# A planned instruction order replaced by another: attention with a position bias and a two-layer MoE-style MLP on one core

## The chip, the cores and the metric

The kernel runs on one core of one Trainium2 chip. The metric is the time of one execution on the device in microseconds (us), of which the median of three runs is taken. Engines are named as the profile names them: PE is TensorE (PEld its weight loads), DVE is VectorE, ACT is ScalarE, POOL is GpSimd, SP is SyncE, which here only issues DMA transfers.

## What is computed

The reference, cut to what matters (4 batches, 8 heads, 576 positions, 64 values per head; 2304 tokens, 512 and 2048 features):

```python
scores = scale * np.matmul(q, k.transpose(0, 1, 3, 2))
x = (log1p(abs(i - j)) / log1p(max(i, 1)))[..., None]
bias = np.maximum(x @ w1 + b1, 0.0) @ w2          # hidden size 32, one value per head
scores = scores + bias.transpose(2, 0, 1)[None]
attn = np.exp(scores - np.max(scores, axis=-1, keepdims=True))
attn = attn / (np.sum(attn, axis=-1, keepdims=True) + 1e-09)
x = np.matmul(attn, v)                              # heads side by side: 2304 x 512
h = np.maximum(x @ w_in, 0.0)
out = h * h @ w_out
```

## The kernel before

The work is cut into ten blocks, each a pair of batches and one 128-row slice of positions (two of the ten hold the last 64 rows of both batches), and each block into eight heads: 80 attention steps in all. Most products are done in three 16-bit passes, since every float32 operand is split into a high and a low half.

One kind of work follows another, and each is a small generator function named by a two-letter word:

- The bias table. hgen (hg) makes the hidden layer of the bias for four rows at a time from a table of logarithms (lines 469 to 477, on ACT or DVE), bias_mm (bm, L542) multiplies by w2 on PE, bias_out (bo, L568 to L573) scales the result and writes rows to memory (L579, L583), and bias_ld (bl, L603, L607) reads them back as a tile bt for one head. Before any of this stand w2s and sclw (scales, sc, L947 and L949), which come from a small input tensor sm_t and the table tab_t.
- The weights. w_dma (wd, L346 and L349) loads 32 blocks of 512 KB of w_in and w_out as 64-bit floats into a tile stg; w_split (ws) turns each into float32 with three DVE instructions (L362, L364, L369: tiles ci and cv) and then into two 16-bit halves on ACT and POOL.
- The attention step. qk (L623, L637) makes scores on PE in a PSUM tile sc; softmax_a (sa) adds the bias and finds the maximum on DVE (L656) and takes the exponential on ACT (L667, L669); softmax_b (sb) splits the result on ACT and POOL (L276, L710, L712) into a tile a and transposes it by a DMA on SP's queue into a tile at (L719); pv (L757) multiplies by v. The first 16 steps are transposed on PE instead (turn, tu).
- The end of a block. pv_out (po), norm (no) and turn_x (tx) scale the result, split it (L818, L820: tile xh) and transpose it by DMA (L825) into a tile xt.
- The MLP. g1 (L837) is one eighth of the first layer for a block, 24 matmuls; square (sq) takes relu and square on ACT and DVE and splits on DVE and POOL (tile g); g2 (L872) adds to the second layer, six matmuls for each half of a block; store (ou) writes the result.

Every engine runs its instructions in the order in which they are written, and that order is a list of words: the string PROGRAM. Each word is a generator and its arguments, and each time the word appears the generator is driven one step further. "ws:4" for instance stands six times, once for each step of the split of block 4. At the end of the program every instruction is tied to the one before it on its engine, so no scheduler changes the order:

```python
for word in PROGRAM.split():
    if word not in live:
        kind, _, arg = word.partition(":")
        live[word] = iter(work[kind](*[int(x) for x in arg.split(".") if x]) or ())
    next(live[word], None)
```

All DMA transfers but the last one are issued on SP's queue, in the order of the list; a transfer that has to wait for its data or its buffer holds up those behind it. The string HID names for each of 36 groups of bias rows an entry of PATS, which says which of the four hidden tiles of a group is made on which engine (A for ACT, D for DVE, P for POOL). HID holds only the digits 0, 1 and 2.

Of the kernel before, what the change touches and what calls it, by code (L numbers as in the profile page):

```python
# [8 lines left out]
F32 = mybir.dt.float32  # L9
# [3 lines left out]
AF = mybir.ActivationFunctionType  # L13
ALU = mybir.AluOpType
# [11 lines left out]
LW = 576  # L26
# [4 lines left out]
PATS = ["DDDD", "ADDD", "AADD", "DDDP", "DDPP", "ADDP", "ADPP", "AADP", "AAPP", "DPPP"]  # L31
# [170 lines left out]
def tile_attention_moe(  # L202
# [11 lines left out]
    nc = tc.nc  # L214
# [44 lines left out]
    sel = const.tile([128, 32], F32, name="sel")  # L259
    rows_s = const.tile([128, 36], F32, name="rows_s")  # L260
    nb1 = const.tile([128, 1], F32, name="nb1")
    hcst = const.tile([128, 4], F32, name="hcst")

    eps = const.tile([128, 2], F32, name="eps")
    esc = const.tile([128, 1], F32, name="esc")
# [172 lines left out]
    def pat(gi):  # L438
        return PATS[int(HID[gi])]

# [577 lines left out]
```

## Time and profile before

| what | value |
|---|---|
| median of three runs | 636.6 us (635.3 to 640.33) |
| the profiled execution, its own time | 637.86 us |
| its span, first to last instruction | 636.1 us |
| mean granted TensorE clock | 0.981 |
| busy: PE, DVE, ACT, POOL | 597.7, 428.1, 366.5, 385.4 us |
| DMA | 112.19 MB, mean 176 GB/s |

Busy time is the time in which at least one instruction of the engine runs. The ends of matmuls are modelled, and matmuls overlap, so a row's mean is longer than the distance from one to the next; how long a group of matmuls takes is read from the chain of work, which is given in pieces of equal instructions that follow each other. Of the 637.86 us, 1.76 lie around the span.

### The profile page before, as it was taken

Reading aid. Unit: us, or ns where it says so; the run is one execution under the profiler, and the core shown is the slowest. Engines: PE = TensorE matmul, PEld = TensorE weight load, DVE = VectorE, ACT = ScalarE, POOL = GpSimd, SP = SyncE. Lnnn points to the kernel's source line nnn. Section 1 sums busy time; section 2 is a strip of 40 time slices with the busy share of each in tenths; the row PEclk is TensorE's granted clock in tenths of the full one; section 3 lists DMA queues with packets and bytes.
Section 4 is the critical chain, followed back from the end, with each engine's and each line's share of the span. In section 5 each row is a group of like instructions: output and inputs, shape, how many; then the busy total and the mean of one; then the engine's idle time right before and its main releaser. Section 6 shows DMA issues by size and latency. Waiting matters only on the chain.

```text
span 636.1 us, 15958 instructions
## 1 busy us (share of the span) xinstructions
PE 597.7 (94%) x6296; PEld 402.7 (63%) x6296; DVE 428.1 (67%) x840; ACT 366.5 (58%) x779; POOL 385.4 (61%) x389
## 2 busy tenths in 40 slices
PE   5658998899999999999999999999999999999997
PEld 2124576475767467667657865767676686577576
DVE  7988999899669796787974663566456463613321
ACT  5559997687777465645567455746636574214020
POOL 5766499989767435866866647555665555523221
PEclk9669999899999999999999999999999999999999
DMA  8999987778979969799789969559955787623000
GB/s 291 325 285 284 286 237 253 244 188 203 191 183 185 220 159 170 184 226 221 177 164 219 165 131 186 139 115 196 186 136 122 158 169 144 140 34 72 18 34 18
DMA packets 204426, 112.19 MB, mean 176 GB/s; under 512 B 166848, under 2 KB 179392, under 8 KB 204352
## 3 DMA queue, kind: packets, MB, share of 16 engines
q1 hardware_dynamic: 204272, 111.12, 75.2%
q8 instruction: 49, 0.80, 0.5%
q14 instruction: 25, 0.20, 0.1%
q10 hardware_dynamic: 80, 0.07, 0.0%
HBM read 55.44 MB, written 15.61 MB: 112 GB/s over the span
## 4 chain that ended last, share of the span: by engine, by line
PE 51%; DMA 5%; DVE 5%; POOL 4%; issue 3%; ACT 2%; SPq 1%; POOLq 0%; DVEq 0%; ACTq 0%
PE hp L837 20%; PE o L872 19%; PE pv L757 5%; PE sc L637 5%; DMA at<-a 3%; DMA xt<-xh 2%; POOL a L712 2%; PE bp L542 1%; DVE s L656 1%; POOL g L857 1%; DVE g L280 1%; ACT s L669 1%; DMA stg<-vd 1%; DVE r L851 1%; ACT a L276 1%
## 5 line engine op out<-in xcount | busy, mean ns | idle before, releaser
L837 PE MATMUL hp<-xt,winH 128*128 128x256 f16 (+1 forms) x1280 | 193.3, 262 | 2.0 <-DVE r L851 1.1
L872 PE MATMUL o<-woutH,g 128*128 128x512 f16 (+1 forms) x608 | 186.4, 369 | 2.2 <-POOL g L857 1.6
L837 PE MATMUL hp<-xt,winL 128*128 128x256 f16 (+1 forms) x640 | 161.7, 262 | 0.0
L857 POOL TENSOR_TENSOR g<-r,g 128x512 f16<-128x512 f32 (+1 forms) x80 | 88.4, 1108 | 88.3 <-DVE g L280 81.5
L872 PEld LDWEIGHTS <-g 128*128 128x128 f16 x912 | 84.3, 98 | 90.5 <-issue 4.5
L712 POOL TENSOR_TENSOR a<-s,a 128x1024 f16<-128x1024 f32 (+1 forms) x64 | 133.1, 2079 | 0.0
L837 PEld LDWEIGHTS <-winH 128*128 128x128 f16 x1280 | 117.8, 98 | 20.6 <-DVE r L851 1.2
L656 DVE CUSTOM_DVE_ANT_0 s<-sc,bt 128x576 f32<-128x576 f32 x144 | 104.6, 749 | 35.7 <-PE sc L637 15.2
L851 DVE TENSOR_TENSOR r<-hp,r 128x512 f32<-128x512 f32 (+1 forms) x80 | 50.7, 634 | 105.6 <-ACT r L849 105.2
L872 PE MATMUL o<-woutL,g 128*128 128x512 f16 (+1 forms) x304 | 112.1, 369 | 0.0
L669 ACT ACTIVATE s<-s,nm 128x576 f32<-128x576 f32 x120 | 92.9, 774 | 6.6 <-ACT nm L667 0.4
L710 POOL TENSOR_TENSOR a<-s,a 128x128 f16<-128x128 f32 (+1 forms) x64 | 30.3, 473 | 105.6 <-ACT a L276 73.7
L849 ACT ACTIVATE r<-hp 128x512 f32<-128x512 f32 (+1 forms) x80 | 43.7, 546 | 85.4 <-PE hp L837 75.2
L757 PE MATMUL pv<-v,at 128*128 128x64 f16 (+5 forms) x2112 | 87.8, 203 | 1.9 <-ACT at L276 1.2
L667 ACT ACTIVATE nm<-mx,esc 128x1 f32<-128x1 f32 x120 | 34.4, 287 | 84.2 <-DVE mx L656 84.0
L276 ACT ACTIVATE a<-s 128x1152 f16<-128x1152 f32 (+1 forms) x64 | 70.3, 1098 | 14.6 <-DMA at<-a 13.5
L837 PEld LDWEIGHTS <-winL 128*128 128x128 f16 x640 | 62.6, 98 | 5.8
L757 PEld LDWEIGHTS <-at 128*128 128x128 f16 (+1 forms) x1792 | 55.0, 100 | 10.4 <-issue 3.6
L477 DVE TENSOR_SCALAR hg<-tab_t 128x464 f32<-128x464 f32 (+17 forms) x88 | 60.9, 723 | 0.7 <-PE bp L542 0.6
L280 DVE TENSOR_SCALAR g<-r 128x512 f16<-128x512 f32 (+1 forms) x64 | 48.0, 754 | 18.4 <-PE o L872 17.4
L637 PE MATMUL sc<-k,q 64*128 64x128 f16 (+1 forms) x768 | 58.2, 284 | 1.3 <-DVE mx L656 1.2
L637 PEld LDWEIGHTS <-q 64*128 64x128 f16 x768 | 39.6, 94 | 28.1 <-issue 19.0
(88 smaller groups left out, 687.1 us busy)
## 6 DMA issues: line engine op xcount, KB each, us to landing
bt<-biasd SPq DMA_DIRECT2D x64, 288.0 KB, 3.5
stg<-w_in SPq DMA_DIRECT2D x16, 512.0 KB, 6.0
stg<-w_out SPq DMA_DIRECT2D x16, 512.0 KB, 5.5
biasd<-be SPq DMA_DIRECT2D x16, 295.5 KB, 6.2
bt<-biasd SPq DMA_DIRECT2D x32, 144.0 KB, 4.7
qst<-qd SPq DMA_DIRECT2D x32, 128.0 KB, 3.3
out<-o SPq DMA_DIRECT2D x16, 256.0 KB, 2.5
v<-vd SPq DMA_DIRECT2D x8, 320.0 KB, 7.0
```

The source lines that it names most:

```text
L276: nc.scalar.activation(out=out, in_=in_, func=AF.Copy, scale=scale)
L280: nc.vector.tensor_scalar(out, in_, scale, None, op0=ALU.mult)
L477: nc.vector.tensor_scalar(ht, src, scl[:, n:n + 1], None, op0=ALU.min)
L637: i = nc.tensor.matmul(out=sc[:, o:o + w], lhsT=qt[r, qz, qs], rhs=kt[r, z, k0:k0 + w], start=(m == 0), stop=(m == 2), tile_position=(64 * ...
L656: nc.vector.tensor_tensor_reduce(s[:, 576 * b:576 * b + 576], sc[:, sb:sb + 576], bt, inv, 3.0e38, ALU.add, ALU.min, mx[:, b:b + 1])
L669: nc.scalar.activation(out=sl, in_=sl, func=AF.Exp, scale=-1.0, bias=mx[:, b:b + 1] if f32 else nm[:, b:b + 1], accum_out=su[:, h, b:b + 1])
L712: eng.tensor_tensor(av[:, :, 640:1152], ev[:, :, 0:512], av[:, :, 0:512], op=ALU.subtract)
L757: nc.tensor.matmul(out=dst, lhsT=lhsT, rhs=rhs, start=b not in [x[1] for x in seq[:j]], stop=b not in [x[1] for x in seq[j + 1:]], tile_po ...
L837: nc.tensor.matmul(out=hp[:, f * T:f * T + T].rearrange("p (b t) -> p b t", b=nb), lhsT=wt[:, k, c0:c0 + 128], rhs=xt[:, 0:nb, z * 4 + k, ...
L851: nc.vector.tensor_tensor(rr, hp[:, 0:2 * T], rr, op=ALU.mult)
L857: eng.tensor_tensor(g[:, 1, 0:2 * T], rr, g[:, 0, 0:2 * T], op=ALU.subtract)
L872: nc.tensor.matmul(out=blk["o", b][:, 0:256] if halved else blk["o", b], lhsT=g[:, z, c0:c0 + 128], rhs=wt[:, 2 * u + f, d], start=(u == 0 ...
```

## The change

The list PROGRAM is written anew. It holds the same words the same number of times (2555 of 2556; the one that is gone drove a generator that had already ended), and the instructions of each engine are the same in kind, shape and number. Three small edits go with it: PATS loses the seven entries behind its third and gets two others, of which HID uses none; the branch in hgen for POOL, which only those entries reached, is taken out; and the negated w1 gets a tile of its own, nw1, where it was a column of hcst, which is now five columns wide.

```diff
-PATS = ["DDDD", "ADDD", "AADD", "DDDP", "DDPP", "ADDP", "ADPP", "AADP", "AAPP", "DPPP"]
+PATS = ["DDDD", "ADDD", "AADD", "AAAD", "AAAA"]
 HID = '112211111122222222222211111111110000'
...
-    "st tb:1 qd:0 st st tb:0 st st st st st st st qd:0 qd:0 qd:0 kd:0.0 wd:0 rs sc wd:1 sc hc sc sc hg:1.0 rs "
...
-    hcst = const.tile([128, 4], F32, name="hcst")
+    hcst = const.tile([128, 5], F32, name="hcst")
+    nw1 = const.tile([128, 1], F32, name="nw1")
...
-            elif pat(gi)[t] == "P":
-                nc.gpsimd.tensor_scalar(ht, src, scl[:, n:n + 1], 1.0, op0=ALU.min, op1=ALU.mult)
...
-        nc.scalar.activation(out=tab_t[:, 0:LW], in_=tab_t[:, 0:LW], func=AF.Identity, scale=hcst[:, 3:4], bias=0.0)
+        nc.scalar.activation(out=tab_t[:, 0:LW], in_=tab_t[:, 0:LW], func=AF.Identity, scale=nw1, bias=0.0)
...
-        nc.vector.tensor_scalar(hcst[:, 3:4], sm_t[:, 0:1], -1.0, None, op0=ALU.mult)
+        nc.vector.tensor_scalar(nw1, sm_t[:, 0:1], -1.0, None, op0=ALU.mult)
```

The new list begins "st tb:1 qd:0 st wd:0 st st st st st st st tb:0 kd:0.0 kd:0.1 wd:1". In the changed kernel line numbers are one higher from the new tile on up to hgen (L299 becomes L300, L471 becomes L472) and one lower behind the branch that is taken out (L477 becomes L476, L719 becomes L718).

What stands on SP's queue at the start, before (tab_t is the table, sm_t the small tensor, stg a weight block, kst a head of k, qst the first queries, v a head of v):

```order
L942 DMA tab_t<-tabs 128x720
L944 DMA sm_t<-sm 128x34
L416 DMA qst<-qd 64x4x64 x2
L299 DMA kst<-kd 128x576
L346 DMA stg<-w_in 128x2x256 x2
L299 DMA kst<-kd 128x576
L346 DMA stg<-w_in 128x2x256
L321 DMA v<-vd 128x640 x6
```

The same stretch of SP's queue in the changed kernel:

```order
L941 DMA tab_t<-tabs 128x720
L347 DMA stg<-w_in 128x2x256
L943 DMA sm_t<-sm 128x34
L300 DMA kst<-kd 128x576 x2
L347 DMA stg<-w_in 128x2x256
L417 DMA qst<-qd 64x4x64
L347 DMA stg<-w_in 128x2x256
L417 DMA qst<-qd 64x4x64
L322 DMA v<-vd 128x640 x6
```

The first weight block has moved in front of the small tensor, both first heads of k in front of the queries, and the second and third weight blocks to either side of the first half of the queries.

DVE's first rows before (hg is a hidden tile of the bias, ci the first step of a weight split, w2s and sclw the scaled weights of the bias, rows_s a small constant, nb_135 the negated bias):

```order
L947 TENSOR_SCALAR w2s<-sm_t 128x32
L949 TENSOR_SCALAR sclw<-tab_t,sm_t 128x16
L951 TENSOR_SCALAR nb_135<-sm_t 128x1
L953 TENSOR_SCALAR hcst<-sm_t 128x1
L500 COPY rows_s<-cp 128x36
L471 TENSOR_SCALAR hg<-tab_t,sclw,nb_135 128x544
L488 COPY hcst<-cp 128x1 x2
L502 RECIPROCAL tab_t<-tab_t 128x144
```

DVE's first rows in the changed kernel:

```order
L499 COPY rows_s<-cp 128x36
L363 TENSOR_SCALAR ci<-stg 128x512
L946 TENSOR_SCALAR w2s<-sm_t 128x32
L948 TENSOR_SCALAR sclw<-tab_t,sm_t 128x16
L950 TENSOR_SCALAR nb_135<-sm_t 128x1
L365 SCALAR_TENSOR_TENSOR ci<-stg,ci 128x512
L501 RECIPROCAL tab_t<-tab_t 128x144
L472 TENSOR_SCALAR hg<-tab_t,sclw,nb_135 128x560
```

The first step of a weight split, which reads the first weight block, has moved ahead of w2s and sclw, and the second step ahead of the first hidden tile.

SP's queue around the 65th to 68th attention step, before (at is a transposed attention tile, xt a transposed block for the MLP, bt a head's bias):

```order
L719 DMA_TRANSPOSE at<-a 128x18x128
L825 DMA_TRANSPOSE xt<-xh 128x8x128
L719 DMA_TRANSPOSE at<-a 128x18x128
L825 DMA_TRANSPOSE xt<-xh 128x8x128
L607 DMA bt<-biasd 128x576
L416 DMA qst<-qd 64x4x64 x2
L907 DMA out<-o 128x512
L719 DMA_TRANSPOSE at<-a 128x18x128
```

The same steps on SP's queue in the changed kernel:

```order
L718 DMA_TRANSPOSE at<-a 128x18x128
L606 DMA bt<-biasd 128x576
L718 DMA_TRANSPOSE at<-a 128x18x128
L417 DMA qst<-qd 64x4x64
L824 DMA_TRANSPOSE xt<-xh 128x8x128
L606 DMA bt<-biasd 128x576
L417 DMA qst<-qd 64x4x64
L718 DMA_TRANSPOSE at<-a 128x18x128
```

The store of a result and one of the two block transposes no longer stand between the attention transposes here; on PE the first-layer steps of the MLP that used to lie among these steps have moved behind them.

## Rows read from the trace of the kernel before

**Rows 1.** The page: busy time, share of the span and instructions of each engine.

```profile
PE 597.7 (94%) x6296; PEld 402.7 (63%) x6296; DVE 428.1 (67%) x840; ACT 366.5 (58%) x779; POOL 385.4 (61%) x389
```

**Rows 2.** Busy time by stretch: us, PE, PEld, DVE, ACT, POOL busy (xcount), PEclk, DMA share, GB/s.

```profile
0.00:160.00 160.00, 129.03 (x1211) 77.38 (x1212) 146.95 (x288) 120.70 (x263) 123.97 (x151) 0.93 0.89 259
160.00:632.00 472.00, 468.70 (x5087) 325.30 (x5085) 280.99 (x553) 245.79 (x517) 261.40 (x239) 1.00 0.72 149
...
20.00:40.00 20.00, 11.24 (x38) 1.85 (x38) 18.45 (x29) 9.17 (x17) 16.06 (x17) 0.61 1.02 277
```

**Rows 3.** Waits of PE from 160 us on: us in total, times, longest.

```profile
PE hp L837 <- DVE r L851: 1.1, 1, 1.1
PE hp L837 <- DMA xt<-xh: 0.9, 3, 0.6
PE o L872 <- POOL g L857: 0.6, 1, 0.6
```

**Rows 4.** Waits of DVE from 0 to 160 us.

```profile
DVE w2s L947 <- DMA sm_t<-sm: 3.0, 1, 3.0
DVE s L656 <- DMA bt<-biasd: 1.5, 1, 1.5
DVE s L656 <- DMA stg<-w_out: 1.4, 1, 1.4
DVE ci L362 <- DMA stg<-w_out: 1.4, 2, 1.1
DVE ci L362 <- DMA stg<-w_in: 0.9, 2, 0.5
DVE q L428 <- POOL q L278: 0.9, 1, 0.9
```

**Rows 5.** DVE in order of time: start, us, instruction [idle before it <- releaser].

```profile
38.05 0.69 DVE L362 TENSOR_SCALAR ci<-stg 128x512 uint32<-128x512 uint32 x1 [0.55 <-DMA stg<-w_in]
...
50.42 0.69 DVE L362 TENSOR_SCALAR ci<-stg 128x512 uint32<-128x512 uint32 x1 [1.15 <-DMA stg<-w_out]
```

**Rows 6.** PE and DVE in order of time: their first uses of the loaded tensors.

```profile
3.99 0.35 PE L496 MATMUL cp<-tab_t,sel 128*32 128x36 f32 x8 [3.99 <-DMA tab_t<-tabs]
4.05 0.18 DVE L947 TENSOR_SCALAR w2s<-sm_t 128x32 f32<-128x32 f32 x1 [3.04 <-DMA sm_t<-sm]
```

**Rows 7.** Busy time by stretch, the first 8 us (the last column is GB/s).

```profile
0.00:4.00 4.00, 0.01 (x2) 0.04 (x3) 0.15 (x4) 1.49 (x2) 1.56 (x10) 1.00 0.40 109
4.00:8.00 4.00, 1.05 (x17) 0.57 (x18) 3.87 (x16) 3.59 (x5) 1.61 (x3) 1.00 0.94 291
```

**Rows 8.** DMA issues: xcount, KB each, median us from issue to landing.

```profile
stg<-w_in SPq DMA_DIRECT2D x16, 512.0 KB, 6.0
...
xt<-xh SPq DMA_TRANSPOSE x18, 3.8
```

**Rows 9.** Groups of instructions: the first step of a weight split (busy us, mean ns).

```profile
L362 DVE TENSOR_SCALAR ci<-stg 128x512 uint32<-128x512 uint32 x32 | 22.0, 688 | 2.5 <-DMA stg<-w_out 1.4 <-DMA stg<-w_in 0.9
```

**Rows 10.** The chain that ended last, in order of time: start, us, piece.

```profile
241.53 0.92 PE bp L542 x8
...
251.56 1.29 PE o L872 x6
252.86 2.62 PE hp L837 x24
...
256.77 0.84 PE sc L637 x10
...
263.88 0.83 PE pv L757 x28
```

**Rows 11.** The last pv and the issue of the last block's transpose, in order of time.

```profile
593.43 1.07 PE L757 MATMUL pv<-v,at 128*64 128x64 f16 x56
...
597.41 1.23 SPq L825 DMA_TRANSPOSE xt<-xh  x1
```

**Rows 12.** SP: all attention transposes (ns min/median/max), and one bias load (start, us).

```profile
L719 SPq DMA_TRANSPOSE at<-a x64: 1244/2776/5248, 135.8 to 585.6; - x64
...
28.56 0.48 SPq L603 DMA_DIRECT2D bt<-biasd  x1
```

295 rows, old and new, of the table PROGRAM are left out of this document.

## The prediction

> **What bounds the kernel now.** I read the page first: PE is busy for 597.7 of 636.1 us [rows 1], far ahead of DVE's 428.1, so the next question is whether that holds in every stage. The table by stage says no [rows 2]. In the first 160 us PE is busy for 129.03 us and DVE for 146.95; from 160 to 632 us PE is busy for 468.70 of 472 us and DVE for 280.99. So there are two stages: DVE sets the pace of the first (it splits the weights, makes the bias tables and does the first softmax steps), and PE sets that of the second, which is as good as full. The waits of PE after 160 us confirm it: the three rows of it sum to 2.6 us [rows 3]. What the program's order can change is therefore small and known: PE's 31 us without work before 160 us, its 3.3 us in the second stage, and the 4 us behind the last matmul, which no order removes, since the last result must be scaled and stored.
>
> The waits of DVE in the first stage come next [rows 4]. It waits 3.0 us for its first input, and then for DMA: 1.5 us for a bias row (bt), 1.4 us put down to a w_out transfer before a softmax, 1.4 us for w_out blocks and 0.9 us for w_in blocks in its splits. Four of these, 3.4 us together (0.55, 1.48, 0.24 and 1.15), lie between 38 and 51 us; the first and the last are shown [rows 5]. In that stretch DMA and not DVE is late. TensorE's granted clock falls to 0.61 from 20 to 40 us [rows 2], where PE has little to do and DVE is busy for 18.45 of 20 us; a slower PE costs nothing there.
>
> **The change part by part.** The operations are the same; what is moved is the place of each on its engine. The list of hidden-layer patterns loses entries, but the string that picks from it holds only 0, 1 and 2, and those three are unchanged. That edit therefore moves no row between engines and costs nothing. The separate tile for the negated w1 is the same one-column write as before.
>
> *The start.* Before, SP issues the tables and the small tensor first and DVE's first real work is w2s and sclw, at 4.05 us, right after both have landed [rows 6]. Now SP puts the first 512 KB of w_in between the two, and DVE has the first step of that block's split (ci) in front of w2s, sclw and nb1. All bias work hangs on sclw, so it now hangs on the landing of w_in. When is that? In the first 4 us DMA moved 109 GB/s, 0.44 MB, and after that 291 GB/s [rows 7]. The tables (360 KB) and the block are 0.87 MB, so the rest of 0.43 MB takes 1.5 us: landed at 5.5 us, 1.4 us later than DVE's start at 4.05. The two ends: nothing, if the block lands with the tables, and 3.2 us, if it takes the 6.0 us that the w_in issues take as a median [rows 8] from an issue at 1.3 us. I take 1.4, the one that is worked out from the bytes moved in this stretch. The step itself (0.69 us [rows 9]) is work that was due anyway, but sclw is 1.4 + 0.7 = 2.1 us late.
>
> *What hides it.* DVE's waits for DMA between 38 and 51 us. If DVE arrives later it waits less, as long as DMA has not become later as well. I counted both in the two orders. Ahead of DVE's first softmax stand 35.3 us of DVE work before and 33.1 us now (each row by the mean of its form); the bias row that this softmax reads is complete after 10.49 MB of transfers before and 10.22 MB now. Ahead of the fourth w_out split stand 14.62 and 14.33 MB, 57 and 56 transfers. So the queue is 0.29 MB shorter at the place where DVE waits for it, at 291 GB/s 1.0 us. I take a gain of 1.0 us for the whole start, with the late sclw hidden; the ends are 3.4 us of gain (all four waits go) and 3.9 us of loss (3.2 + 0.7, nothing hidden).
>
> *From 50 to 160 us.* Here the order decides how much PE work stands ready per DVE work. Up to DVE's 288th instruction, the count at 160 us [rows 2], the order before has 213 matmuls of the first layer, and that after 240; the second layer has 48 in both, scores 156 in both, bias 120 against 116. By the pieces of the chain (24 first-layer matmuls in 2.62 us [rows 10]) 27 more are 2.9 us, less 0.4 us for four bias matmuls (eight in 0.92 us, the same group): 2.5 us ahead. At the 250th instruction the lead is nothing and at the 320th 0.9 us, so it is not steady. I take half, 1.2 us; the ends are 0 and 2.5 us.
>
> *From 160 us on.* PE has only 3.3 us to lose or to win. In front of each attention product (pv) and each second-layer step stands as much other PE work as before or more (from a block's first-layer step to its second-layer step 20.7 us on average against 18.1, in pieces of rows 10), so I count 0. The ends are a gain of 2.6 us (rows 3 gone) and the loss in the last rival.
>
> *The end.* After the last pv comes a serial chain: scale, norm, split of x, transpose. Its transpose is issued 2.9 us after pv's end at 594.5 us [rows 11] and lands 3.8 us later [rows 8], 6.7 us in all. Before, six second-layer pieces of 1.29 us [rows 10], 7.7 us, cover it; now there are five, 6.45 us. That leaves 0.3 us open. Behind the last first-layer step there are now ten pieces instead of eight, which closes a gap of 0.4 us at 628 to 632 us. I count 0 for both.
>
> The sum: 637.86 us (the profiled execution, 636.1 of it the span) - 1.0 - 1.2 = 635.7. That execution was 1.26 us above the median of the three runs, 636.6, so the median should come to 634.4 us. That is 0.3% less. A measurement of this kernel tells about 1% from no change, so it would read as the same.
>
> **The rivals.** *All waits of the first stage go.* DVE's five waits behind its start, 1.5 + 1.4 + 1.4 + 0.9 + 0.9 for a copy of q made on POOL, are 6.1 us [rows 4]; with the full lead of 2.5 us the time would be 636.6 - 8.6 = 628.0. For it: an order made with the durations of this kernel can place each load earlier. Against it: the positions of the loads relative to DVE's work differ by less than 0.3 MB at most of the places counted, and DMA's share in that stretch is already full (1.02 from 20 to 40 us [rows 2]).
>
> *The late start is not hidden.* w_in lands at 7.3 us, the bias tables are 3.9 us later, and the first softmax waits for the bias chain, not for bytes: 636.6 + 3.9 = 640.5. For it: the bias rows are written to memory and read back, so the bt load cannot be issued before its tables are done. The Trainium skill, "DMA: Bandwidth & Descriptors", section "Queues, rings and completion order", says that on each DMA engine descriptors are consumed in ring order; by that the small tensor and both first k loads start behind 512 KB, 1.8 us at 291 GB/s, and the time would be 636.6 + 1.8 + 0.7 - 1.2 = 637.9. The trace agrees in so far as the small tensor, issued behind the tables, was used 0.06 us after them [rows 6].
>
> *SP's queue becomes the bound in a dense stretch.* The ten score steps from the 60th to the 70th head stood among 73.5 us of PE work; now they stand among 47.6 us (8 first-layer steps, 9 second-layer pieces, 8 pv, 10 score steps, by rows 10). Each head needs one transpose and one bias load on SP. A transpose issue takes SP 1.24 to 5.25 us with a median of 2.78, a bias load 0.48 [rows 12]. At the median that is 3.3 us per head, inside the 4.76 us that PE now takes per head; at the longest it is 5.73, and ten heads lose 9.7 us: 634.4 + 9.7 = 644.1, slower than before. It decides from an issue of 4.3 us on. Against it: the long issues of the trace include waits for POOL and ACT, and PE has further work behind the stretch that does not need these heads.
>
> **How the numbers follow.** The forecast of 634.4 us has a chance of 0.56, with its own range of 630.5 to 638.5; all waits gone 0.20; start not hidden 0.12; SP bound 0.12. The range reaches down past 628.0 and up past 640.5 but not to 644.1: 627 to 643, which leaves out that rival and a little below. More than 1% faster means under 630.2: the first rival and a little of the forecast, 0.22. More than 1% slower means over 643.0: 0.10. The rest, 0.68, is the same.
>
> **What would show it right or wrong.** In the changed profile PE should again be busy for over 99% from about 160 us to the end. DVE's first wait should end at about 5.5 us on w_in; its DMA waits between 38 and 51 us should come to about 2.4 us or less. First-layer matmuls begun by 160 us should number 210 to 240. The step on the start is wrong if DVE's work at 50 us is more than 2 us behind; the step from 160 us on is wrong if PE's idle time there is over 6 us; SP's rival shows as PE waits on transposes (at) between about 440 and 500 us.

## The result, and the profile after

| | before | after |
|---|---|---|
| median of 12 runs each | 637.03 us | 641.49 us |
| ratio, 95% interval | | 1.0087 (1.0065 to 1.0109) |
| the profiled execution: own time, span | 637.86, 636.1 us | 644.93, 643.2 us |

The changed kernel is 0.9% slower by the ratio, some 5.5 us; the two medians lie 4.5 us apart. A second measurement, in the runs below, gave 1.0105 (1.0073 to 1.0136). The forecast was 634.4 us and "the same"; the time lies inside its range, on the other side of no change. The profiled execution is 3.4 us above the median of the changed kernel, as that of before is 0.8 us above its own, so the two spans overstate the difference.

The page, busy time, share of the span and instructions (it answers to [rows 1]):

```profile
PE 598.1 (93%) x6296; PEld 405.1 (63%) x6296; DVE 421.1 (65%) x840; ACT 367.3 (57%) x779; POOL 381.9 (59%) x389
```

PE is busy for 0.4 us more than before, and the mean granted clock is 0.981 in both profiles. Of the 7.1 us that the two spans differ, 6.7 are idle time of PE, and the table by stage says where (columns as in [rows 2]; the idle time of a stage is its length less PE's busy time):

```profile
0.00:160.00 160.00, 130.20 (x1223) 80.80 (x1224) 146.66 (x286) 119.81 (x262) 125.63 (x152) 0.93 0.88 258
160.00:632.00 472.00, 460.48 (x5002) 317.75 (x5001) 272.54 (x550) 246.62 (x516) 254.93 (x235) 1.00 0.72 150
...
274.00:356.00 82.00, 77.38 (x806) 53.37 (x805) 55.44 (x101) 45.78 (x95) 55.95 (x54) 1.00 0.98 203
...
480.00:560.00 80.00, 75.22 (x877) 53.91 (x875) 42.41 (x87) 42.71 (x91) 39.46 (x39) 1.00 0.80 153
```

Up to 160 us PE has done 1.2 us more than before. From 160 to 632 us it is idle for 11.5 us instead of 3.3. The same two stretches of the kernel before:

```profile
274.00:356.00 82.00, 80.08 (x832) 54.97 (x830) 60.28 (x106) 47.34 (x99) 57.49 (x54) 1.00 0.96 196
...
480.00:560.00 80.00, 79.78 (x904) 54.38 (x902) 44.05 (x89) 41.37 (x90) 44.90 (x43) 1.00 0.72 145
```

So 2.7 us of new idle time lie between 274 and 356 us and 4.6 between 480 and 560 us. PE's waits from 160 us on, after (they answer to [rows 3]; us in total, times, longest):

```profile
PE sc L636 <- DVE mx L655: 4.5, 5, 1.6
PE o L871 <- POOL g L856: 2.9, 4, 1.4
PE pv L756 <- DMA at<-a: 2.3, 3, 1.3
PE hp L836 <- DVE r L850: 1.1, 1, 1.1
PE o L871 <- DVE g L281: 0.7, 1, 0.7
```

PE waits for three engines, which suggests that none of these is the origin. What they wait for in turn shows from 260 us on, in the waits of ACT and of DVE:

```profile
ACT a L277 <- DMA at<-a: 23.6, 15, 4.8
...
DVE s L655 <- POOL a L711: 15.2, 4, 5.1
```

The same rows of the kernel before:

```profile
ACT a L276 <- DMA at<-a: 13.5, 7, 3.4
...
DVE s L656 <- POOL a L712: 2.5, 2, 2.2
```

The chain can be read in one place, in order of time over all engines: steps 67 to 71 of the attention, which the new order runs close together.

```profile
491.59 1.15 ACT L277 ACTIVATE a<-s 128x1152 f16<-128x1152 f32 x1
495.28 2.38 POOL L711 TENSOR_TENSOR a<-s,a 128x1024 f16<-128x1024 f32 x1
497.00 1.16 ACT L277 ACTIVATE a<-s 128x1152 f16<-128x1152 f32 x1
498.73 3.49 SPq L718 DMA_TRANSPOSE at<-a  x1
...
506.10 1.16 ACT L277 ACTIVATE a<-s 128x1152 f16<-128x1152 f32 x1 [4.78 <-DMA at<-a]
507.73 2.13 POOL L711 TENSOR_TENSOR a<-s,a 128x1024 f16<-128x1024 f32 x1
509.90 0.76 DVE L655 CUSTOM_DVE_ANT_0 s<-sc,bt 128x576 f32<-128x576 f32 x1 [5.13 <-POOL a L711]
510.41 1.16 POOL L856 TENSOR_TENSOR g<-r,g 128x512 f16<-128x512 f32 x1
511.62 0.60 PE L871 MATMUL o<-woutH,g 128*128 128x512 f16 x2 [1.45 <-POOL g L856]
```

There are two tiles a. ACT takes the first for step 67 at 491.59 and the second for step 68 at 497.00; for step 69 it needs the first again, whose transpose was issued at 498.73; ACT starts at 506.10, when it has landed, 7.4 us later. That tile was held for 14.5 us: besides its own work it waited 2.2 us for POOL and 1.1 us for SP. POOL's second half of the split follows ACT; DVE's softmax of step 71 waits for POOL, because there are two score tiles s; POOL's work for the MLP (g) stands behind that split on its queue; and PE waits for g. One late transpose has become a wait of PE on POOL, 13 us later and in another kind of work.

DVE's start went as forecast. DVE's first rows after (they answer to [rows 6]), and its waits for DMA up to 160 us (to [rows 4]):

```profile
5.38 0.69 DVE L363 TENSOR_SCALAR ci<-stg 128x512 uint32<-128x512 uint32 x1 [0.58 <-DMA stg<-w_in]
5.99 0.17 DVE L946 TENSOR_SCALAR w2s<-sm_t 128x32 f32<-128x32 f32 x1
6.07 0.23 DVE L948 TENSOR_SCALAR sclw<-tab_t,sm_t 128x16 f32<-128x16 f32 x1
```

```profile
DVE s L655 <- DMA bt<-biasd: 1.8, 2, 0.9
...
DVE ci L363 <- DMA stg<-w_in: 0.6, 1, 0.6
DVE ci L363 <- DMA stg<-w_out: 0.6, 1, 0.6
DVE cv L370 <- DMA biasd<-be: 0.5, 1, 0.5
```

### The profile page after: what moved, and what is told of

It is laid out like the page before. It is cut to its first block, busy times and chain, and to the rows that moved or that the text cites. A ratio compares the mean times of both kernels' runs of the same rounds, so it can differ in the third digit from the quotient of the medians.

```text
span 643.2 us, 15951 instructions
## 1 busy us (share of the span) xinstructions
PE 598.1 (93%) x6296; PEld 405.1 (63%) x6296; DVE 421.1 (65%) x840; ACT 367.3 (57%) x779; POOL 381.9 (59%) x389
## 4 chain that ended last, share of the span: by engine, by line
PE 61%; DMA 12%; DVE 11%; POOL 7%; issue 4%; ACT 3%; SPq 1%; DVEq 0%; POOLq 0%; ACTq 0%
PE o L871 23%; PE hp L836 22%; PE pv L756 7%; DMA at<-a 5%; PE sc L636 5%; PE bp L541 3%; DMA biasd<-be 3%; POOL g L856 2%; DVE s L655 2%; POOL a L711 2%; DMA bt<-biasd 1%; DVE hg L476 1%; DVE hg L472 1%; DVE ci L363 1%; DMA stg<-w_out 1%
## 5 line engine op out<-in xcount | busy, mean ns | idle before, releaser
L655 DVE CUSTOM_DVE_ANT_0 s<-sc,bt 128x576 f32<-128x576 f32 x144 | 105.1, 751 | 48.1 <-POOL a L711 15.2
L476 DVE TENSOR_SCALAR hg<-tab_t 128x464 f32<-128x464 f32 (+17 forms) x88 | 56.1, 666 | 1.5 <-PE bp L541 1.2
L281 DVE TENSOR_SCALAR g<-r 128x512 f16<-128x512 f32 (+1 forms) x64 | 38.2, 599 | 23.2 <-PE o L871 22.2
```

Source lines behind the costliest of these rows:

```text
L476: nc.vector.tensor_scalar(ht, src, scl[:, n:n + 1], None, op0=ALU.min)
L655: nc.vector.tensor_tensor_reduce(s[:, 576 * b:576 * b + 576], sc[:, sb:sb + 576], bt, inv, 3.0e38, ALU.add, ALU.min, mx[:, b:b + 1])
```

## The experiments

All are the changed kernel with another list, or the list with one buffer or some bytes changed; code is shown in short form. Line numbers are those of the changed kernel. The table gives each run's ratio to the kernel before (its 95% interval) and, from its profile, PE's idle us in four stretches; what the columns say is told run by run below it.

| run | ratio | 160-274 | 274-356 | 356-480 | 480-560 |
|---|---|---|---|---|---|
| before | 1 | 0.1 | 1.9 | 0.6 | 0.2 |
| after | 1.0087 (1.0065-1.0109) | 1.3 | 4.6 | 0.8 | 4.8 |
| e9, after again | 1.0105 (1.0073-1.0136) | 1.5 | 4.5 | 1.4 | 3.5 |
| e1, new first part | 1.0024 (1.0005-1.0044) | 1.4 | 0.7 | 1.2 | 0.6 |
| e2, new middle | 1.0080 (1.0062-1.0099) | 0.1 | 5.9 | 1.4 | 0.0 |
| e3, new last part | 1.0102 (1.0063-1.0142) | 0.1 | 1.7 | 1.9 | 2.8 |
| e4, old last part | 1.0063 (1.0041-1.0086) | 1.5 | 5.0 | 1.1 | 0.0 |
| e8, old middle | 1.0087 (1.0055-1.0118) | 1.9 | 0.6 | 2.1 | 3.5 |
| e5, few bytes | 1.0038 (1.0018-1.0058) | 0.7 | 1.3 | 0.7 | 2.4 |
| e10, old order, few bytes | 0.9978 (0.9960-0.9997) | 0.1 | 0.6 | 0.7 | 0.2 |
| e11, few bytes from step 32 on | 1.0026 (1.0000-1.0051) | 1.4 | 1.2 | 0.9 | 1.9 |
| e12, old order, extra bytes | 1.0070 (1.0043-1.0098) | 0.1 | 3.8 | 0.5 | 0.3 |
| e6, bias loads on ACT's queue | 1.0080 (1.0051-1.0108) | 1.1 | 4.2 | 1.1 | 3.9 |
| e7, DVE's softmax first | 1.0182 (1.0144-1.0220) | 0.7 | 7.2 | 1.5 | 3.5 |
| e13, three tiles a | 1.0065 (1.0043-1.0087) | 1.8 | 1.9 | 0.8 | 1.4 |
| e14, old order, three a | 0.9994 (0.9970-1.0018) | 0.1 | 1.6 | 0.6 | 0.3 |
| e15, three tiles s | 1.0109 (1.0082-1.0136) | 0.7 | 4.8 | 0.9 | 3.3 |
| e16, three s, few bytes | 1.0064 (1.0043-1.0085) | 0.8 | 1.5 | 1.0 | 2.2 |
| e17, three a, transpose earlier | 1.0081 (1.0051-1.0111) | 0.8 | 3.1 | 1.6 | 1.8 |
| e18, all three | 1.0024 (1.0004-1.0044) | 0.8 | 0.8 | 1.0 | 1.6 |

**Where: e1 to e4 and e8.** At the 36th step (about 274 us) both orders have done the same words but for six, at the 47th (356 us) but for fourteen. The lists can be cut and joined there: each joined list takes one order up to a cut and then, from the other, the words that are not yet done, in its order.

```diff
-PROGRAM = new
+PROGRAM = new up to qk:36, then what is left of old        # e1
+PROGRAM = old up to qk:36, new up to qk:47, rest of old    # e2
+PROGRAM = old up to qk:47, rest of new                     # e3
+PROGRAM = new up to qk:47, rest of old                     # e4
+PROGRAM = new up to qk:36, old up to qk:47, rest of new    # e8
```

> The new order up to the 36th attention step (about 274 us, where both orders have done almost the same words), the old order from there on. The output is the reference's. Theory A (the loss lies in the dense stretches behind it): PE's idle time up to 274 us is made good by the first-layer work done earlier, so 637 us within 1.5 us of before, and PE waits behind 274 us come to 2 us or less, as before. Rival B (the new start costs the time, through the late bias scale and the lower clock at 100 to 120 us): the whole loss is here, 640.5 to 641.5 us. Rival C (the loss is spread evenly, through transposes that take SP longer everywhere): 274 of 640 us, so about 1.9 us, 639 us.

> The old order, but from the 36th to the 47th attention step (about 274 to 356 us) the new one. The output is the reference's. Theory A: the profile after shows 2.7 us more PE idle time in this stretch than the profile before, so 638.5 to 639.7 us, with PE waits on DVE's maximum (scores) in the trace between 280 and 330 us. Rival B: 637 us, no such waits. Rival C: 82 of 640 us, 0.6 us, 637.6 us.

> The old order up to the 47th attention step (about 356 us), the new one from there to the end. The output is the reference's. Theory A: the profile after shows 4.8 us more PE idle time here than the profile before, most of it between 490 and 556 us, so 639.5 to 641.8 us, with PE waits on POOL's g and DVE's r there. Rival B: 637 us. Rival C: 280 of 640 us, 2 us, 639 us, with waits all along.

> The new order up to the 47th attention step (about 356 us), the old one from there to the end. The output is the reference's. Theory A: the stretches add up, so this is e1 and e2 together, 638 to 640 us, and what is missing to 641.5 us is the loss of the last stretch. Rival B: 640.5 to 641.5 us. Rival C: 639.5 us.

> The new order, but from the 36th to the 47th attention step (about 274 to 356 us) the old one. The output is the reference's. If the stretches add up without joins: 641.5 less the 2.2 us that lie between e4 and e1, 639.3 us. If the old middle keeps DMA below its full share only because the old last stretch follows, PE's idle time from 356 us on grows over the 4.8 us of the profile after, and the time stays at 641 us or more.

The new first part costs 1.5 us (0.3 to 2.8), not the whole loss: rival B falls. Rival C, an even spread, falls with all three of e1 to e3, which lie 2 us or more from its values. The new middle alone costs 5.1 us and the new last part alone 6.5 us, each with PE's idle time in its own stretch as theory A has it, but each more than its share: the three parts sum to 2% where the whole is 0.9%. The parts do not add up. A cut of the old order followed by the new also has its own losses: e3 has 1.9 us idle behind the join where before has 0.6. e8 takes the middle's waits away (0.6 us idle instead of 4.6) and is no faster than the whole new order; its idle time behind 356 us is that of the profile after, 5.6 us in both, so what its expectation named for that case, more idle time there, is not the reason. So these runs locate the waits but don't price them.

**Bytes or queues: e5, e6, e7.** In e5 the bias loads of the dense stretches bring 64 of 576 columns, as often as before, and the softmax reads these nine times over; in e6 they are issued by ACT; in e7 DVE's softmax stands ahead of the splits of k and v.

```diff
+            w = 64 if n in (36..46, 64..71) else S
-            nc.sync.dma_start(out=t, in_=rows(...))
+            nc.sync.dma_start(out=t[:, 0:w], in_=rows(...)[:, 0:w])               # e5
+            (nc.scalar if n in (36..46, 64..71) else nc.sync).dma_start(...)       # e6
-PROGRAM: ... qk:38 ou:2.0 sb:37 vs:1.1 g2:23 sb:36 sa:38 vs:1.1 sb:37 sa:38 ...
+PROGRAM: ... qk:38 sa:38 sa:38 ou:2.0 sb:37 vs:1.1 g2:23 sb:36 vs:1.1 sb:37 ...  # e7, steps 37 to 44
```

> The new order, unchanged, but for the attention steps 36 to 46 and 64 to 71 (the two dense stretches) the bias load brings 64 of 576 columns, and the softmax reads these nine times over; the output of these heads is therefore not the reference's. SP issues as many transfers, in the same places, DVE does the same work, and 18 x 256 KB fewer are moved. Theory D (DMA is full in the dense stretches, 1.0 to 1.1 of its share from 260 to 320 us against 0.63 to 0.99 before from 290 to 330, and 1.0 from 500 to 520 us; transposes land late, buffers come free late, DVE and POOL pass it on to PE): PE's idle time from 274 to 356 us falls from 4.6 to 2.5 us or less, from 480 to 560 us from 4.8 to 2.5 or less, and the time to 637 to 638.5 us. Rival Q (the loss is made by the place of instructions on DVE's and SP's queues, whatever the bytes): idle time as in the profile after, 641 us.

> The new order, but the bias loads of steps 36 to 46 and 64 to 71 are issued on ACT's queue, at the same place of the list. The output is the reference's; bytes are unchanged. Rival S (SP's queue is too full in the dense stretches, as the last rival of the prediction has it): SP is free of 0.5 us and of a buffer's wait per head, PE's idle time behind 274 us falls by half, 638 to 639 us. Theory D: the bytes still stand in front of the transposes, 641 us, idle time within 1.5 us of the profile after.

> The new order, but for the attention steps 37 to 44 DVE's two softmax instructions stand right behind the scores (qk) of the same step, ahead of the k and v splits and of the MLP's r that they stood behind. The output is the reference's. Theory Q (PE waits on DVE's maximum because these stand in DVE's queue behind splits that wait for POOL or are stretched by it): the waits of PE's scores on DVE's maximum between 274 and 356 us fall from 3.9 us to 1 us or less, and the time to 638.5 to 639.5 us. Theory D: these waits stay over 2.5 us or come back as others, 640.5 to 642 us.

Fewer bytes take the middle's idle time from 4.6 to 1.3 us and that of the last stretch from 4.8 (3.5 in e9) to 2.4; the time falls to 0.4% over before, 638.06 us, within what theory D expected. DMA's share shows what changed, from 274 to 356 us of e5 (the column before the last, 0.98 in the profile after):

```profile
274.00:356.00 82.00, 80.73 (x871) 57.03 (x870) 55.13 (x103) 48.45 (x103) 56.27 (x55) 1.00 0.84 176
```

Taking the bias loads off SP does nothing (e6). The transposes stay on SP, but in the ten steps of the prediction's last rival each took SP 2.7 to 3.6 us in the profile after, under the 4.3 us from which that rival decides: it falls in its own form. e7 misses both expectations. The waits on DVE's maximum do go, from 3.9 to 0.7 us, but they come back larger, as waits for the MLP's r, and the kernel is 1.8% slower than before:

```profile
PE hp L836 <- DVE r L850: 5.2, 2, 3.5
PE o L871 <- POOL g L856: 1.3, 2, 0.8
PE sc L636 <- DVE mx L655: 0.7, 1, 0.7
```

DVE then waits at the head of its queue for a free score tile (23.6 us behind POOL's split from 260 us on, 15.2 after), with r behind it. So the place on DVE's queue matters, and theory Q's repair is no repair.

**Controls: e9 to e12.**

```diff
+            w = 64 if n in (36..46, 64..71) else S      # e10, with the old list
+            w = 64 if n >= 32 else S                    # e11, with the new list
+            for z in ([t, spare] if n in (36..46, 64..71) else [t]):
-            nc.sync.dma_start(out=t, in_=rows(...))
+                nc.sync.dma_start(out=z, in_=rows(...)) # e12, with the old list
```

> The changed kernel itself, unchanged, for a second profile beside the runs of this study. The profile after was of an execution 3.4 us above the median. Expected: 641 us, 0.9% over before; the waits of PE behind 274 us at the same places (scores near 287 and 320 us, second-layer steps near 512 and 552 us), their sum 7 to 10 us.

> The old order with the same reduced bias loads as in the run with few bytes (64 of 576 columns for steps 36 to 46 and 64 to 71, read nine times over; the output of these heads is not the reference's). The control to that run. Theory D (DMA decides only where the new order crowds the heads): 635.5 us within 1 us, PE's idle time behind 274 us about 2.5 us as before. Rival (fewer bytes help any order): 2 to 3 us faster than before, 632.5 to 633.5 us.

> The new order with the reduced bias loads for all steps from 32 on (64 of 576 columns, the output of these heads is not the reference's). Theory D for the whole loss behind 274 us: the 2.4 us that the run with few bytes in two stretches kept over before fall to 1 us or less (635.5 to 636.5 us), and the waits for g near 552 us go. If the rest is made by the order on DVE, ACT and POOL: 637.5 to 638.5 us, waits for g and r between 500 and 556 us stay.

> The old order, with each bias load of steps 36 to 46 and 64 to 71 followed by a second one of the same bytes into a spare tile that nothing reads (18 x 288 KB more, about 18 us of all DMA engines). The output is the reference's. Theory D: the stretches of the old order become as crowded as the new order's, transposes land later, PE waits for DVE's maximum, g or pv's transposed tile between 274 and 356 and between 480 and 560 us: 2 to 6 us slower than before, 637.5 to 641.5 us. Rival (bytes don't matter, SP's issues neither): 635.5 to 636.5 us.

e9 shows the same stalls at the same places. The old order, too, gains 1.4 us by the ratio (0.2 to 2.5) from fewer bytes, 633.54 us as a median: beyond what theory D left it and next to what the rival gave. Held against this control, the new order with few bytes is still 0.6% behind (1.0038 less 0.9978, 3.8 us), where the whole is 6 us: bytes account for some 2 us (1.7 against the first measurement of the new order, 2.9 against the second, each give or take more than 2). e12 shows the reverse: with extra bytes, and an extra issue on SP for each, the old order loses 4.4 us, and its idle time from 274 to 356 us doubles from 1.9 to 3.8, though its profile is of the fastest of its ten executions. What bytes don't explain is plain in e11. Its time, 637.44 us, lies between the two cases expected, next to the one in which the order makes the rest. Without nearly all bias bytes behind step 32, DVE still waits for the score tile as long as after:

```profile
DVE s L655 <- POOL a L711: 16.2, 5, 4.4
```

**The ring: e13 to e16.** One more buffer for one tile each:

```diff
-    a_p = pool("a", 2)
+    a_p = pool("a", 3)     # e13 new list, e14 old list
-    w_p = pool("w", 2)
+    w_p = pool("w", 3)     # e15 new list, e16 with few bytes as in e5
```

> The new order with three buffers instead of two for the softmax halves (the tile a, which is held from ACT's split until its transpose has landed). Theory R (the new order runs the heads at 4.3 to 4.8 us in its dense stretches, but two tiles a, each held for about 1.2 + 2.6 us of splitting, SP's wait and 4.7 to 7.3 us until the transpose has landed, allow one head per 4.8 to 6 us; ACT's wait for a tile a passes on to POOL, to the score tile s and to DVE): ACT's waits for at<-a from 260 us on fall from 23 to under 8 us, DVE's for s (POOL a) from 15.6 to under 5, and the time to 637 to 639 us. Theory D alone (bytes): DMA is as full as before, transposes land as late, 640.5 us or more.

> The old order with three tiles a: the control. Theory R: the old order hardly waits for them (13.5 us of ACT, 2.5 us of DVE, none of it passed on to PE), 635.4 us within 1 us. If a third tile helps any order by the same, 2 us or more faster, 633.5 us or less.

> The new order with three buffers instead of two for the scores (the tile s). DVE then doesn't wait for POOL's split of the head before the last: its waits for s fall from 15.6 us to under 3. ACT still waits for a tile a as long (over 15 us). If it is DVE's place (MLP instructions queued behind the waiting softmax) that PE feels: 637.5 to 639.5 us. If it is the transposes behind it: 640.5 us or more.

> The new order with three score tiles s and the reduced bias loads of steps 36 to 46 and 64 to 71 (64 of 576 columns; the output of these heads is not the reference's). Both theories together: PE's idle time from 274 to 560 us falls to 3 us or less and the time to 634.5 to 636 us, within 2.5 us of the old order with the same few bytes (633.5 us). If something else of the new order costs the rest: 637 to 638 us, as with few bytes alone.

With a third tile a no wait of ACT for at<-a is left behind 260 us, DVE's wait for s is halved, from 15.6 to 7.7 us (theory R had under 5), and PE's idle time in the two stretches falls from 8.0 us (e9) to 3.3, although DMA moves the same bytes; in e17, which has three tiles a too, it is 4.8. From 274 to 356 us and from 480 to 560 us of e13:

```profile
274.00:356.00 82.00, 80.07 (x835) 55.48 (x836) 54.98 (x102) 45.83 (x96) 58.20 (x57) 1.00 0.93 202
...
480.00:560.00 80.00, 78.59 (x892) 56.09 (x891) 43.14 (x86) 41.53 (x88) 40.22 (x40) 1.00 0.75 144
```

What the ring does shows in ACT's rows for the first half of a, at the 64th and at the 72nd step, first after, then e13:

```profile
476.81 1.16 ACT L277 ACTIVATE a<-s 128x1152 f16<-128x1152 f32 x1
...
522.03 0.68 ACT L277 ACTIVATE a<-s 128x576 f16<-128x576 f32 x1 [3.75 <-DMA at<-a]
```

```profile
474.59 1.16 ACT L277 ACTIVATE a<-s 128x1152 f16<-128x1152 f32 x1
...
512.55 0.68 ACT L277 ACTIVATE a<-s 128x576 f16<-128x576 f32 x1
```

The eight steps take 45.2 us with two tiles and 38.0 with three: one step in 5.65 and in 4.74 us.

The time follows less clearly, 1.0065 instead of 1.0087 and 1.0105, so 1.4 to 2.5 us. The intervals overlap, e17 stands at 1.0081, and 639.66 us misses theory R's 637 to 639. So the third tile's effect on the waits is shown, its price in time is not. The same tile does nothing for the old order (e14), as theory R has it; this run carries the three small edits too, so they cost nothing that can be measured. A third tile s takes DVE's waits for it from 15.6 to 5.4 us (under 3 expected), leaves ACT's for at<-a at 23.2 us and gives nothing (e15). With few bytes, e16, it gives nothing beyond them and misses both of its cases. The score tile only passes the wait on, the tile a makes it.

**Adding up: e17 and e18.** In the first part PE waits 0.7 to 1.5 us at about 165 us for one transpose. In SP's queue, after, it stands behind two stores and two loads, while its data are complete when POOL ends at 157.3 us (the last row):

```profile
156.18 1.19 SPq L910 DMA_DIRECT2D out<-o  x2
157.47 0.54 SPq L582 DMA_DIRECT2D biasd<-be  x1
158.10 1.38 SPq L419 DMA_DIRECT2D qst<-qd  x2
159.58 4.19 SPq L718 DMA_TRANSPOSE at<-a  x1
...
154.76 2.58 POOL L711 TENSOR_TENSOR a<-s,a 128x1024 f16<-128x1024 f32 x1
```

```diff
-hg:24.0 sb:18 hg:24.1 sb:18 po:4 bm:24.0 ou:0.0 ou:0.0 ... po:4 g1:10 sq:8 sb:18
+hg:24.0 sb:18 hg:24.1 sb:18 sb:18 po:4 bm:24.0 ou:0.0 ou:0.0 ... po:4 g1:10 sq:8
-    a_p = pool("a", 2)
+    a_p = pool("a", 3)     # e17; e18 with few bytes as in e5 in addition
```

> The new order with three tiles a, and in addition one transpose (that of attention step 18) moved on SP's queue from behind two stores, a bias row and two loads of q to ahead of them. The output is the reference's. In the profiles with the new first stretch PE waits 0.7 to 1.5 us for this transpose at 164 to 166 us, and 160 to 274 us holds 1.3 us more idle time than in the old order. If that is the whole loss of the first stretch: the wait is gone, idle time from 160 to 274 us is 0.5 us or less, and the time is 1.3 us below that with three tiles a alone, 0.45% over before (638.3 us). If the start itself is late: 639.5 us, with the wait gone or not.

> The same with the reduced bias loads of steps 36 to 46 and 64 to 71 in addition (64 of 576 columns; the output of these heads is not the reference's): bytes, ring and the late transpose all taken away. If these three are the loss: 633.5 to 635.5 us, within 2 us of the old order with the same few bytes (633.5 us); what stays is the wait for DVE's maximum near 286 us and for g near 506 to 550 us, 1 to 2 us. If there is a further cause: 637 us or more.

The wait at 165 us goes in both, idle time there falls to 0.8 us (0.2 to 0.4 us waits for r stay), and the time does not show it: e17 lies above e13, the intervals overlap. Of its two cases 640.32 us is nearer to the one in which the start itself is late (639.5 against 638.3), so a late start stays possible as the loss of the first part. e18, with bytes, ring and late transpose taken away, is 0.46% over its control e10 (2.9 us, give or take 1.7 by the two intervals), where the whole was 6. Its 636.97 us stand at the edge of the case with a further cause (637 or more): about half of the loss is accounted for by the three, and half is not. Against few bytes alone (e5, 1.0038) the tile and the transpose bring 0.14%, within the noise. The profile of e18, of the slowest of its 13 executions, shows where the other half is at least in part: 4.1 us idle from 160 to 560 us against 1.5 in e10, in waits of 0.3 to 1.0 us at six places, the longest on a transpose at 426 us and on g near 550 us. Waits at these two places, 0.7 to 1.0 and 0.9 to 1.6 us, stand in every profile with the new last part; no run took them away.

The first of them points to a ring that was not tried. The tile at, which the transpose writes and pv reads, has two buffers as well, and SP waits for pv before a transpose. From 160 to 560 us, before, after and in e18:

```profile
SPq L719 <- PE pv L757: 5.9, 5, 2.7
```

```profile
SPq L718 <- PE pv L756: 34.1, 10, 9.6
```

```profile
SPq L718 <- PE pv L756: 24.7, 10, 9.6
```

The longest wait of the two new ones is for the transpose that PE waits for at 426 us. In the profile after its data are complete at 410.75 us, and it is issued at 419.77, as soon as a pv that stands behind first-layer matmuls has run; PE itself then waits 0.8 us for it. A run with a third tile at is missing, so what this ring costs is not known. No version of the new order here is faster than the kernel before.

## Why the prediction was wrong

*The start* was right in its rows. The first weight block was used at 5.38 us (5.5 forecast), and DVE's waits for DMA between 38 and 51 us came to 0.86 and 0.57 us, 1.4 in all (2.4 or less forecast): the late bias scale was hidden where the prediction said, DVE's first softmax began at 37.7 us instead of 41.0, and a start 3.9 us late, as that rival had it, does not show. The rival with all waits gone falls with the result.

*From 50 to 160 us* the profile has 227 first-layer matmuls begun by 160 us, within the 210 to 240 named, and 1.2 us more PE work in all, the value taken. That this pair of profiles shows the value is luck. By 160 us PE is idle for 30.9 us on average in the six profiles with the old first part and for 30.7 in the fourteen with the new, and has begun 1219 and 1223 matmuls: four are 0.4 us, by 24 in 2.62 us. So the 1.0 and 1.2 us that the sum takes off are not seen. By 274 us the new first part is behind by 21 matmuls on average, but by 6 as a median, so by some 2 us at most; e1 measures a loss of 1.5 us. PE's wait of 1.3 us at 165 us, for the transpose behind the stores, is of this size, but that it is the loss was not shown (e17).

*"From 160 us on … I count 0"* is the step that failed, by the prediction's own mark of 6 us of idle time (11.5 in this profile). It was argued from PE work in front of each attention product on average. That is the cover that a step has on PE; it says nothing of how many steps the other resources can hold at once. A first bound was in the trace before. A tile a is held for ACT's split, 1.16 us, POOL's, 0.43 + 2.13, and the transpose until it lands, 4.7 us as a median before: 8.4 us, and more by each wait in SP's queue. With two tiles that is one step in 4.2 us at the very best. The new order asks for one in 4.76 us, as the prediction worked out for steps 60 to 70, which leaves 1.1 us of a tile's turn of 9.5 for waits. In these ten steps of the profile after a tile was held for 8.8 to 14.4 us, 10.4 on average: two tiles allow one step in 5.2 us, and the steps came one in 5.5. With three tiles (e13) ACT waits for none, and steps 64 to 71 came at the asked pace, 4.74 us. The bytes have a part in it: the ten transposes landed after 5.5 us on average, 5.1 with few bytes (e5) and 5.0 before. The averages over all steps hid ten steps in a row. The middle's waits fell with fewer bytes and with the third tile (e5, e13), but how much of the 6 us each of the two costs is not settled.

*The rival on SP's queue* named one of the two stretches and the sign, with the wrong resource. It priced the transpose by SP's issue (3.3 us per step) and not by the time until it lands, and it looked for waits on at between 440 and 500 us. e6 shows that SP's issues of bias loads are not the bound; the waits that cost most there came from 511 us on, on g and on DVE. Its objection, that PE has other work behind the stretch, failed because, in the chain above, that work waits on POOL behind the softmax steps.

*The end* was within 1 us of the 0 counted: behind 560 us PE is idle for 3.7 us, 0.9 less than before.

The Trainium skill, "Perfetto Trace Analysis", section "Optimization Strategy", says that consistent bubbles on the engine that should be saturated can mean that there isn't enough SBUF for the next tile to be allocated, by the buffer count. The third tile a agrees, with 8.0 us of idle time against 3.3 (4.8 in e17). What the trace adds is that PE's gaps here are not consistent: they are single waits on three engines, and only ACT's row names the tile a.

## What to carry to other kernels

For an order that packs steps closer together, work out for each tile that goes round in a ring how long one buffer is held, from its first write until the last reader or transfer has landed, with the waits in the queues between (here 8.4 us without them and 10.4 with), and divide by the number of buffers; no stretch may ask for steps faster than that, whatever the average. Do the same with the bytes of a step against what DMA moves, in the densest stretch. When the waits of the bound engine point to several engines at once, follow the waits of those engines until one names a transfer or a buffer.

## What the runs showed that was not expected

Executions of one kernel differ by more than the effect: the changed kernel ran from 639.81 to 646.61 us, and PE's idle time before 160 us was 28.9 to 33.2 us in six profiles of the same first part. A profile pair alone would have said 1.1%, and a single profile of e13 (636.0 us of span) would have said no loss at all.

A DVE split of v takes 0.82 us at the least and 2.75 at the most. The longest, with POOL's split beside it, stands in front of the two softmax instructions whose maximum PE waited for at 287 us:

```profile
282.90 2.75 DVE L336 SCALAR_TENSOR_TENSOR v<-stg,v 128x640 f16<-128x640 f32 x1
...
282.32 2.65 POOL L711 TENSOR_TENSOR a<-s,a 128x1024 f16<-128x1024 f32 x1
...
287.06 0.91 PE L636 MATMUL sc<-k,q 64*128 64x128 f16 x12 [1.39 <-DVE mx L655]
```

POOL's instruction ends at 284.97 us, DVE's 0.68 us later: it looks as if the whole of DVE's work came behind POOL's. The Trainium skill, "SBUF — State Buffer", section "SBUF: two separate sides", says that a DVE operation with two SBUF inputs and a GpSimd operation that reads SBUF lock a shared pair of ports for the whole instruction, and the other fully blocks. The two rows agree with it; no run here took the overlap away. That the ring of a delays the steps is shown by a third buffer (e13, e14), and that bytes cost time by fewer and by more of them (e5, e10, e12). The remaining 2.9 us stay open, with the ring of at as an untested candidate.
